# Seven block products for eight in the gates of the last 2048 tokens and in the output products of the last 1024

## The chip, the core and the metric

The kernel runs on one core of one Trainium2 chip. The metric is device microseconds of an execution; lower is better. The engines of the core are TensorE (PE, matmuls, with weight loads shown apart as PEld), VectorE (DVE), ScalarE (ACT), GpSimd (POOL) and SyncE (SP), which here issues nearly all the loads. All arithmetic is in 32-bit floating point; each wide product is made of three matmuls on a high and a low half in the type fp32r.

## The reference

For 4 batches, 8 heads, 768 positions and 64 values a head, attention over a window of 31 positions and over 24 summaries (of blocks of 32: the maximum of the keys, the mean of the values, with log 32 added to the score). The result, 3072 tokens of 512 values, goes through two gates and two matrices:

```python
scores_s = scale * np.einsum('bhsd,bhnd->bhsn', q, k_sum) + np.log(block)
scores_l = np.where(np.abs(pos[:, None] - pos[None, :]) < 16, scale * q @ k.T, -1e9)
a = softmax(concatenate([scores_l, scores_s]))      # the sum has 1e-9 added
x = a @ concatenate([v, v_sum])                     # 3072 x 512
h = (x @ w1) * (x @ w2) @ w3                        # 512 x 1024 each, 1024 x 1024
out = h @ w_out                                     # 1024 x 512
```

## The kernel before

The tokens are worked through in six **units** of 512. Heads come in four **pairs**, so there are 24 steps of attention, each one pair of one unit. The weights arrive as 64-bit words, are turned into floats on DVE and ACT (L150 to L190) and split into a high and a low half (`low`, L108). w3 and w_out are first folded into one matrix wp of 1024x512 (`fold_weights`, L196, 192 matmuls), eight tiles that stay in SBUF.

`products` (L111) is one wide product: high·high, low·high and high·low into one PSUM bank. `gate` (L427) makes one block of 128 columns of both gates for a unit: two banks of 4 × 3 matmuls; ACT copies the first (L448), DVE multiplies the second into it (L453), ACT casts the high half of the result (L454) and DVE makes its low half (L109). `project` (L459) makes 128 tokens of the output: 8 × 3 matmuls with wp into a bank that ACT copies out and stores itself (L472). A unit is 192 matmuls of gates and 96 of output, all 128x512.

Attention of a pair: scores (L331, 32 matmuls, tile sc), the mask and maximum on DVE (L345), the exponential on ACT (L359), its sum's reciprocal (L364 on POOL, L365 on DVE), the scaling on POOL (L368), then transposes on PE (L388, tile tp) copied to pt (L393, L397), and the product with the values (L408, tile po), which ACT and DVE turn into x (L419, L109). The loads of a pair are q, k (L306, L308) and v (L291) on SP; POOL copies the summary keys into k (L318) and the means of the values into v (L298).

The order of the work is written as a stream: `network` (L504) yields after each wide product, and `run(columns)` (L520) pulls it forward to a given sum of columns. In the first part, up to about 85 us, a table of numbered slots (`WORK`, `FIRST`) starts conversions and the first eight pairs. After it, a loop (L760 to L795) takes two pairs at a time: transposes of the two pairs before, scores of the two now, outputs of the two before, and then `run` for half a unit, 144 matmuls. In that part PE and POOL keep the order in which the program is written, and ACT and DVE do inside each step; SP does what the scheduler puts first. Every engine carries its own instructions out in order, and an SP issue that waits for a buffer holds those behind it.

In PSUM, tag mm has two banks (a gate or an output product each), tag tp two, and the scores have four.

Of the kernel before, what the change touches and what calls it, by code (L numbers as in the profile page):

```python
# [70 lines left out]
def attention_moe(ctx, tc, qG, kW, kT, vP, vW, vB, mask, w1, w2, w3T, wo, out):  # L71
# [17 lines left out]
    DO = out.shape[1]  # L89
    SCALE = 1.0 / math.sqrt(D)  # L90
# [15 lines left out]
    wp = [const.tile([P, 2, DO], F32R, name=f"wp{i}") for i in range(NF)]  # L106
# [142 lines left out]
    def value_means(b, c, raw):  # L249
        if c == 0:  # L250
            vs[b] = sb.tile([P, P], F32, name="vs")
        cols = vs[b][:, c * VC : (c + 1) * VC]
        nc.vector.tensor_reduce(out=cols, in_=raw, op=ALU.add, axis=AX.X)
        nc.vector.tensor_scalar(out=cols, in0=cols, scalar1=1.0 / BLOCK, scalar2=None, op0=ALU.mult)

# [59 lines left out]

    def gather(u, p, k):
# [46 lines left out]
    def invert(mx):  # L363
        nc.gpsimd.tensor_scalar(out=mx[:, 1], in0=mx[:, 1], scalar1=1e-9, scalar2=None, op0=ALU.add)  # L364
# [35 lines left out]
    def outputs(pt, v):  # L400

        po = ps.tile([P, 512], F32, name="po", tag="tp", bufs=2)
# [12 lines left out]
        return po  # L415

# [59 lines left out]
    NU = B * S // U  # L476
    NS = NU * NPAIR
# [25 lines left out]

    def network():  # L504
        for u in range(NU):
# [3 lines left out]
            for t in range(NBLK):  # L509
                yield from project(u, t, hs)  # L510

# [6 lines left out]
    given = [0.0]  # L518

    def run(columns):  # L520

        while given[0] < columns:
            n = next(stream, 0)
            if n == 0:
                return
            given[0] += n

# [30 lines left out]
    coming, loaded, turns, under_way = {}, {}, {}, []  # L558
    for b in range(1, B):
        steps = [(lambda c=c, b=b: load_blocks(b, c), lambda raw, c=c, b=b: value_means(b, c, raw)) for c in range(vB.shape[1])]  # L560
        steps += [
            (lambda p=p, b=b: load_keys(b, p), lambda raw, p=p, b=b: summaries(b, p, raw)) for p in range(NPAIR)
        ]
        if b == 1:
            of_second = steps
            continue
        at = b * BLOCKS // NBLK * NPAIR
        if at - 2 * NPAIR >= 2 * NPAIR:
            for i, some in enumerate((steps[:2], steps[4:6], steps[2:4], steps[6:])):
                turns[at - 2 * NPAIR + 2 * i] = some  # L570
            continue
        for at, step in zip((4, 4, 4, 4, 3, 3, 2, 2), steps):
            coming.setdefault(b * BLOCKS // NBLK * NPAIR - at, []).append(step)

    def prepare(s):
        for work, raw in loaded.pop(s, ()):
            work(raw)
        for load_, work in coming.pop(s, ()):
            loaded.setdefault(s + 1, []).append((work, load_()))

    def load_turn():
        if turns:
            under_way.extend((work, load_()) for load_, work in turns[min(turns)])

    def take_turn(s):
        if s in turns:
            del turns[s]
            for work, raw in under_way:
                work(raw)
            under_way.clear()  # L590
            load_turn()


# [70 lines left out]
    def means():  # L664
# [39 lines left out]
        41: [lambda: fetch_values(6), lambda: fetch_values(7), lambda: fill(6)],  # L704
        46: [lambda: fetch_sums(7)],
        47: [lambda: fill(7)],
        51: [lambda: fetch_sums(6)],
    }
    RATE = 8000
# [49 lines left out]
    with tc.manual_schedule(engines={engines.PE, engines.Pool}):  # L759
        for s in range(NFIRST, NS + 1, 2):  # L760
            now = (s, s + 1) if s < NS else ()
            last = (s - 2, s - 1)
            if s == NFIRST:
                for p in range(s, s + NPAIR):
                    prepare(p)
                load_turn()
# [95 lines left out]
```

## Time and profile before

| what | value |
|---|---|
| three runs | 532.22, 532.48, 535.3 us (median 532.48) |
| profiled execution, its span | 533.5 us, 1.0 above the median |
| PE busy | 511.2 us, 96% |
| DVE, ACT, POOL busy | 240.6, 225.4, 95.9 us |
| wide matmuls by line | 1152 gates, 576 output, 192 folding |
| moved by DMA | 68.78 MB |

The page shows an execution by busy time of each engine, and the chain that ended last; a group of instructions is given by line, engine, operation and tile, with count, busy time, mean duration and the idle time ahead. PE's busy time overlaps its weight loads. A view by windows gives the same for stretches of time, with the granted clock of TensorE and the DMA rate. For a transfer, the last number is the microseconds from its issue to its landing.

### The profile page before, as it was taken

The numbers are of one execution on the slowest core, as the hardware profiler recorded it, in microseconds if no ns is written. First come the engines' busy times: TensorE is split into PE (matmuls) and PEld (weight loads), VectorE is DVE, ScalarE is ACT, GpSimd is POOL, SyncE is SP. The second block draws the span as 40 slices with busy tenths as digits, with TensorE's granted clock in tenths as the row PEclk, the third lists the DMA queues.
The fourth block names the chain that finished last, engine by engine and source line by source line (L and its number), as shares of the span: only waits on it lengthen the run. The fifth ranks groups of instructions, "written<-read, shape, count | busy, mean of one in ns | idle before, by whom it ended". The sixth has DMA issues, their size and how long they took to land.

```text
span 533.5 us, 9766 instructions
## 1 busy us (share of the span) xinstructions
PE 511.2 (96%) x3888; PEld 421.4 (79%) x3888; DVE 240.6 (45%) x667; ACT 225.4 (42%) x627; POOL 95.9 (18%) x158
## 2 busy tenths in 40 slices
PE   1889989999999999999999999999999999999997
PEld 0667767888888888888888888888888888888885
DVE  5889987798534326435244043251042350222210
ACT  5587964674626226135154063361172361222210
POOL 2020635001033202305005014014023031000000
PEclk9989997999999999999999999999999999999999
DMA  8995699804834013453040150050150011100001
GB/s 346 413 411 220 252 325 413 316 2 139 274 131 167 0 55 122 151 172 134 0 177 1 60 195 1 1 177 20 49 187 2 14 69 40 39 3 0 1 20 59
DMA packets 21166, 68.78 MB, mean 129 GB/s; under 512 B 2304, under 2 KB 2432, under 8 KB 18560
## 3 DMA queue, kind: packets, MB, share of 16 engines
q1 hardware_dynamic: 17664, 61.86, 31.6%
q10 hardware_dynamic: 3456, 6.29, 3.1%
q8 instruction: 30, 0.49, 0.4%
q14 instruction: 16, 0.13, 0.1%
HBM read 61.85 MB, written 6.29 MB: 128 GB/s over the span
## 4 chain that ended last, share of the span: by engine, by line
PE 87%; DMA 5%; DVE 4%; ACT 2%; issue 1%; POOL 0%; SPq 0%; POOLq 0%; ACTq 0%
PE mm L113 76%; PE po L408 4%; PE sc L331 4%; DMA rows<-in_vP_dram 2%; PE tp L388 2%; DVE wf L176 2%; DMA wraw<-in_w_dram 1%; DVE w L109 1%; DMA wraw<-in_wo_dram 1%; ACT sm L359 1%; DVE wf L173 1%; ACT wf L164 1%; DVE sm L345 0%; ACT w L190 0%; DVE ks L236 0%
## 5 line engine op out<-in xcount | busy, mean ns | idle before, releaser
L113 PE MATMUL mm<-x,w 128*128 128x512 f32 x1152 | 264.3, 391 | 0.0
L113 PEld LDWEIGHTS mm<-x,w 128*128 128x128 f32 x1152 | 216.5, 188 | 45.3
L113 PE MATMUL mm<-wp,h 128*128 128x512 f32 x576 | 133.3, 390 | 0.0
L113 PEld LDWEIGHTS mm<-wp,h 128*128 128x128 f32 x576 | 107.7, 188 | 22.6
L359 ACT ACTIVATE sm<-sm,mx 128x120 f32<-128x120 f32 x192 | 73.6, 385 | 16.3 <-DVE mx L345 16.3
L453 DVE TENSOR_TENSOR g<-mm,g 128x512 f32<-128x512 f32 x48 | 33.1, 690 | 88.7 <-PE mm L113 85.4
L454 ACT CAST h<-g 128x512 fp32r<-128x512 f32 x48 | 29.5, 618 | 90.6 <-DVE g L453 90.6
L113 PE MATMUL mm<-w,w 128*128 128x512 f32 x192 | 51.2, 419 | 14.8 <-ACT w L190 12.0
L113 PEld LDWEIGHTS mm<-w,w 128*128 128x128 f32 x192 | 37.3, 200 | 25.7 <-ACT w L190 12.7
L364 POOL TENSOR_SCALAR mx<-mx 128x8 f32<-128x8 f32 x24 | 6.8, 283 | 275.5 <-ACT sm L359 275.3
L472 ACT COPY o<-mm 128x512 f32<-128x512 f32 x24 | 14.0, 584 | 82.5 <-PE mm L113 82.5
L397 DVE COPY pt<-tp 120x512 f32<-120x512 f32 x22 | 14.3, 684 | 75.2 <-PE tp L388 75.2
L109 DVE TENSOR_TENSOR h<-g,h 128x512 fp32r<-128x512 f32 x48 | 35.2, 736 | 25.6 <-ACT h L454 25.4
L448 ACT COPY g<-mm 128x512 f32<-128x512 f32 x48 | 28.1, 586 | 39.0 <-PE mm L113 38.4
L298 POOL COPY v<-vs 24x512 f32<-24x512 f32 (+1 forms) x64 | 40.7, 635 | 8.9 <-DMA v<-in_vW_dram 5.9
L345 DVE CUSTOM_DVE_ANT_0 sm<-sc,mask_sb 128x120 f32<-128x120 f32 x192 | 41.1, 274 | 0.0
L359 ACT ACTIVATION_READ_ACCUMULATOR sm<-sm,mx 128x1 f32 x192 | 36.2, 188 | 0.0
L368 POOL TENSOR_TENSOR sm<-sm,mx 128x960 f32<-128x960 f32 x16 | 28.7, 1793 | 5.6 <-DVE mx L365 5.6
L109 DVE TENSOR_TENSOR x<-po,x 128x512 fp32r<-128x512 f32 x24 | 16.6, 690 | 28.6 <-ACT x L419 28.5
L190 ACT CAST w<-wf 128x1024 fp32r<-128x1024 f32 (+1 forms) x22 | 21.3, 968 | 17.3 <-DVE wf L176 17.2
L408 PEld LDWEIGHTS po<-pt,v 120*64 120x64 f32 x768 | 24.5, 141 | 4.0 <-issue 2.5
L408 PE MATMUL po<-pt,v 120*64 120x64 f32 x768 | 26.6, 228 | 0.9 <-POOL v L298 0.5
(35 smaller groups left out, 287.9 us busy)
## 6 DMA issues: line engine op xcount, KB each, us to landing
v<-in_vW_dram SPq DMA_DIRECT2D x24, 512.0 KB, 6.4
wraw<-in_w3T_dram SPq DMA_DIRECT2D x8, 1024.0 KB, 13.0
wraw<-in_w_dram SPq DMA_DIRECT2D x8, 1024.0 KB, 9.3
k<-in_kW_dram SPq DMA_DIRECT2D x20, 368.0 KB, 5.3
raw<-in_kT_dram SPq DMA_DIRECT2D x16, 392.0 KB, 3.7
q<-in_qG_dram SPq DMA_DIRECT2D x24, 256.0 KB, 4.9
raw<-in_vB_dram SPq DMA_DIRECT2D x12, 512.0 KB, 3.8
out_dram<-o ACTq DMA_DIRECT2D x24, 256.0 KB, 2.0
```

The lines of the kernel that those rows point to most:

```text
L109: eng.tensor_tensor(dst, src, hi.bitcast(F32), ALU.subtract)
L113: nc.tensor.matmul(acc, lhsT=a, rhs=b, start=first and i == 0, stop=last and i == len(terms) - 1)
L190: nc.scalar.copy(t[:, 0, some], f[:, some])
L298: nc.gpsimd.tensor_copy(v[at : at + NB, g, blocks], src.unsqueeze(1).broadcast_to([NB, n, P]))
L331: nc.tensor.matmul(sc[h][64 * g : 64 * g + 64, i * KR : (i + 1) * KR], lhsT=q[rows, i * P + 64 * g : i * P + 64 * g + 64], rhs=k[rows, i, ...
L345: nc.vector.tensor_tensor_reduce(out=sm[:, j], in0=sc[h][:, i * KR : (i + 1) * KR], in1=mask_sb[:, 0 if blk == 0 else 2 if blk == BLOCKS - ...
L359: nc.scalar.activation(sm[:, j], sm[:, j], AF.Exp, bias=mx[:, 0, j : j + 1], scale=-1.0, accum_out=mx[:, 1, j : j + 1])
L368: nc.gpsimd.tensor_tensor(sm, sm, mx[:, 2].unsqueeze(2).broadcast_to([P, NI, KR]), ALU.mult)
L408: nc.tensor.matmul(po[cols, at : at + 64], lhsT=v[:KR, g, i, cols], rhs=pt[g][:, (h * NBLK + i) * 64 : (h * NBLK + i + 1) * 64], start=Tru ...
L448: nc.scalar.copy(g, a[:, :U])
L453: nc.vector.tensor_tensor(g, acc[1][:, :U], g, ALU.mult)
L454: nc.scalar.copy(h[:, 0], g)
```

## The change

The last 2048 tokens (units 2 to 5) go through the gates two units at a time. The input of such a pair of units and each 512 columns of the weights are cut into two by two blocks, and their product is made of seven block products of sums and differences where there were eight (`lanes`, k from 0 to 6). The x of these units stays in SBUF in plain floats (xraw, L449, a copy on ACT) and serves as the blocks. The differences of inputs are made on POOL in place (`difference`, L552 to L558), their halves on ACT (L562) and DVE (L118). The differences of weights are made once: POOL sums high and low half (L863 for the gates, L880 for wp), then takes the differences (L600 to L611), ACT casts (L591), DVE makes the low half (L118), and the result is stored in DRAM (L597) as wS (gates) and pS (output), 512 KB each; the plain halves are stored as they are (L853, L856). For each product two of them come back (`flow_in`, L666). `lanes` keeps four banks in the gates (tags mm and tp) and two in the output; each lane takes 6 matmuls of a k in the gates and 12 in the output, and after each k its bank is copied on ACT (k of 0 and 1, L691) or added to an earlier one on DVE (L694, L833). POOL multiplies the two gates (L697, 32 times).

Units 2 and 3 then have the plain output product (`project_split`), with wp read from DRAM; units 4 and 5 have the seven products (`project_fast`), and their output is stored transposed, into a second output that the host turns and appends. Units 0 and 1 stay as they were.

Attention now takes one pair at a time (`lump`): transposes, scores, 12 wide matmuls, outputs, then the rest of the pair's share, by the table `UP_TO`. A table `EXTRA` says at which pair weight sums, input differences and weight loads begin. The block means of values go to DRAM (`keep_means`, L329) and come into v by small transfers on SP (L335) instead of POOL copies; a part of the early pairs keeps the copies. The addition in `invert` moves from POOL to DVE (L385). wp lives in buffers that are given to other tiles later.

The core of the diff:

```diff
+    wS = [[tc.dram_tile([P, 2, KH * FQ], F32, name=f"wS{k}_{q}") for q in range(NQ)] for k in range(NK)]
+    pS = {k: [tc.dram_tile([P, 2, 2 * DH], F32, name=f"pS{k}_{c}") for c in range(NF // 4)] for k in range(2, NK - 1)}
+    pW = [tc.dram_tile([P, 2, DO], F32, name=f"pW{i}") for i in range(NF)]
+    vS = [tc.dram_tile([P, P], F32, name=f"vS{b}") for b in range(B)]
...
+    FIRST_OF_GROUP, LAST_OF_GROUP = (0, 2, 4), (1, 3, 6)
+    def source(k, b):
+        return b[(0, 1, 0, 1, 0, 0, 1)[k]][(0, 0, 0, 1, 0, 1, 0)[k]]
...
+    def difference(k, b):
+        src = source(k, b)
+        if k == 2:
+            nc.gpsimd.tensor_tensor(src, b[0][1], src, ALU.subtract)
+        elif k == 3:
+            nc.gpsimd.tensor_tensor(b[0][1], src, b[0][1], ALU.subtract)
+        elif k == 4:
+            nc.gpsimd.tensor_tensor(src, b[1][1], src, ALU.subtract)
+        elif k == 6:
+            nc.gpsimd.tensor_tensor(src, src, b[0][0], ALU.subtract)
...
+        def finished(k, raw):
+            to = sb.tile([P, 2, 512], F32R, name="sp", **home)
+            nc.scalar.copy(to[:, 0], raw)
+            yield 1
+            low(nc.vector, to[:, 1], raw, to[:, 0])
+            yield 1
+            yield 1
+            yield 1
+            nc.sync.dma_start(to_dram(k), to.bitcast(F32))
...
+        nc.gpsimd.tensor_tensor(a22, a21, a22, ALU.add)
+        yield 1
+        nc.gpsimd.tensor_tensor(a21, a11, a21, ALU.subtract)
+        works.append(finished(2, a22))
+        next(works[0])
+        yield 1
+        nc.gpsimd.tensor_tensor(a11, a22, a11, ALU.subtract)
+        works.append(finished(5, a21))
+        next(works[0])
+        next(works[1])
+        yield 1
+        nc.gpsimd.tensor_tensor(a12, a12, a11, ALU.subtract)
+        yield from staggered([*works, finished(4, a11), finished(3, a12)])
...
+    def flow_in(n):
+        while flow and len(ready) < n:
+            t = sb.tile([P, 2, 512], F32R, name="ws", tag="x", bufs=6)
+            flow.pop(0)(t)
+            ready.append(t)
...
+        banks = [ps.tile([P, 512], F32, name="ln", tag=tag, bufs=bufs) for tag, bufs in tags]
+        for k in range(NK):
+            stationary_of = yield from weights_of(k)
+            for i in range(n):
+                for c in range(steps):
+                    if between and c % KH == 0:
+                        between(k, i * steps // KH + c // KH)
+                    a, m = [stationary_of(i, c, w) for w in range(2)], moving_of(k, c)
+                    terms = [(a[0], m[0]), (a[1], m[0]), (a[0], m[1])]
+                    for j, (x, y) in enumerate(terms):
+                        nc.tensor.matmul(
+                            banks[i][:, :U],
+                            lhsT=x,
+                            rhs=y,
+                            start=c + j == 0 and k in FIRST_OF_GROUP,
+                            stop=c == steps - 1 and j == 2 and k in LAST_OF_GROUP,
+                            skip_group_check=True,
+                        )
+                    if c < steps - 1:
+                        yield 3 * U
+                with tc.high_priority(offset=SOONER):
+                    evacuated(k, i, banks[i][:, :U])
+                yield 3 * U
...
+                if k < 2:
+                    nc.scalar.copy(c11 if k else p1, got)
+                else:
+                    to, more = ((p5, p1), (c12, p1), (c12, c12), (p5, p5), (p1, p1))[k - 2]
+                    nc.vector.tensor_tensor(to, got, more, ALU.add)
+                if k >= 5:
+                    a, b = ((c12, p5), (c11, p1))[k - 5]
+                    nc.gpsimd.tensor_tensor(a, a, b, ALU.mult)
+                    finished.half(r, i, 6 - k, a)
+                finished.after(r, k, i)
...
+        EARLIER = {0: 2, 1: 3, 2: 4, 3: 6}
+        def between(k, j):
+            with tc.high_priority(offset=SOONER // 2):
+                if j == 0:
+                    if k in EARLIER:
+                        for b in blocks:
+                            difference(EARLIER[k], b)
+                    if k + 1 < NK:
+                        coming[:] = [halves(source(k + 1, b), d) for b, d in zip(blocks, whole.moving(k + 1))]
+                if j in (1, 2) and k + 1 < NK:
+                    for work in coming:
+                        next(work, 0)
...
+    def fetch_means(u, p, v):
+        for b, blocks, n in batches(u):
+            for g, at in enumerate((CUT, CUT - 64)):
+                src = vS[b][32 * p : 32 * p + NB]
+                nc.sync.dma_start(v[at : at + NB, g, blocks], src.unsqueeze(1).broadcast_to([NB, n, P]))
...
     def network():
-        for u in range(NU):
+        for u in range(2):
             hs = []
             for f in range(NF):
                 yield from gate(f, xs[u], hs)
             for t in range(NBLK):
                 yield from project(u, t, hs)
+        split = Split()
+        yield from gates(1, split)
+        yield from project_split(1, split)
+        tasks.extend(sums_of_output(c) for c in range(2))
+        whole = Whole(2)
+        yield from gates(2, whole)
+        yield from project_fast(2, whole)
...
+        run(given[0] + 12 * U)
+        with tc.manual_schedule(engines={engines.Activation, engines.DVE}):
+            finish_step(p - 2, pt, **more)
+            if b:
+                expose(0, sm, mx)
+                reduce(u, 1, sc, sm, mx)
+                expose(1, sm, mx)
+                invert(mx)
+                normalize(sm, mx)
+            fill(p + 1)
+            reduce_batch()
+        fetch_values(p)
+        for work in EXTRA.get(p, ()):
+            work()
+        run((given[0] + UP_TO[p]) / 2)
+        load_batch()
+        run(UP_TO[p])
```

**SP at the last pairs of unit 1.** In the loop of before, a step's issues on SP are the two pairs' q, k and v and nothing else:

```order
L306 DMA q_2777<-in_qG_dram 128x512
L308 DMA k_2778<-in_kW_dram 128x736
L306 DMA q_2783<-in_qG_dram 128x512
L308 DMA k_2784<-in_kW_dram 128x736
L291 DMA v_2401<-in_vW_dram 128x1024
L291 DMA v_2407<-in_vW_dram 128x1024
L306 DMA q_3141<-in_qG_dram 128x512
L308 DMA k_3142<-in_kW_dram 128x736
```

At the same place of the change (L317, L319 and L302 are q, k and v, L255 blocks of values, L335 means, L597 stores of weight differences, L666 loads of weight pieces):

```order
L597 DMA wS5_2_108<-sp_2622 128x1024
L597 DMA wS4_2_104<-sp_2708 128x1024
L302 DMA v_2765<-in_vW_dram 128x1024
L666 DMA ws_2773<-wS1_1_91 128x1024
L597 DMA wS3_2_100<-sp_2717 128x1024
L255 DMA raw_2789<-in_vB_dram 128x1024
L255 DMA raw_2791<-in_vB_dram 128x1024
L335 DMA v_2765<-vS2_132 24x4x128 x2
L317 DMA q_2813<-in_qG_dram 128x512
L319 DMA k_2814<-in_kW_dram 128x736
```

Stores and weight loads now stand between the loads of a pair, and each means transfer stands behind the load of its v.

**ACT at the start of unit 1.** In a step of before (the exponentials of a pair, the copies g of the first gate's bank, the casts h, the copy pt of transposes):

```order
L359 ACTIVATE sm_2475,mx_2476<-sm_2475,mx_2476 128x120 x5
L454 CAST h_2628<-g_2613 128x512
L359 ACTIVATE sm_2475,mx_2476<-sm_2475,mx_2476 128x120 x3
L448 COPY g_2645<-mm_2632 128x512
L454 CAST h_2628<-g_2645 128x512
L448 COPY g_2676<-mm_2663 128x512
L454 CAST h_2691<-g_2676 128x512
L448 COPY g_2708<-mm_2695 128x512
```

And in the change, after the last x of unit 0:

```order
L453 CAST x_1867<-po_1850 128x512
L380 ACTIVATE sm_1823,mx_1824<-sm_1823,mx_1824 128x120
L591 CAST sp_1934<-wr_1897 128x512
L380 ACTIVATE sm_1823,mx_1824<-sm_1823,mx_1824 128x120 x3
L591 CAST sp_1944<-wr_1897 128x512
L482 COPY g_1909<-mm_1893 128x512
L380 ACTIVATE sm_1823,mx_1824<-sm_1823,mx_1824 128x120 x4
L488 CAST h_1925<-g_1909 128x512
L591 CAST sp_1978<-wr_1897 128x512
```

The casts into sp, whose buffers hold data to be stored, now stand between the exponentials and the copies g that free a bank.

**PE in the gates of units 2 and 3.** Before, banks of the gates in turn (of the last unit; the gates of every unit read so):

```order
L113 MATMUL mm_4837<-x_4356,w12_919 128x512 x3
L113 MATMUL mm_4837<-x_4376,w12_919 128x512 x3
L113 MATMUL mm_4837<-x_4660,w12_919 128x512 x3
L113 MATMUL mm_4837<-x_4680,w12_919 128x512 x3
L113 MATMUL mm_4854<-x_4356,w12_902 128x512 x3
L113 MATMUL mm_4854<-x_4376,w12_902 128x512 x3
```

In the change, the start of the seven-product gates (ln is a lane's bank, xT an input difference, ws a weight piece, po the output of attention; of the output's eight rows the last is shown):

```order
L636 MATMUL ln_3020<-xT_3036,ws_2767 128x512 x6
L636 MATMUL ln_3021<-xT_3036,ws_2767 128x512 x6
L429 MATMUL po_3069<-pt_2988,v_2765 64x64 x2
L429 MATMUL po_3069<-pt_2989,v_2765 64x64 x2
L636 MATMUL ln_3022<-xT_3036,ws_2769 128x512 x6
L636 MATMUL ln_3023<-xT_3036,ws_2769 128x512 x6
L636 MATMUL ln_3020<-xT_3041,ws_2771 128x512 x6
```

Where before had 12 wide matmuls for one bank, a lane has 6 for one k, and the same bank ln_3020 returns with the next piece after three other lanes; one pair's output stands 12 matmuls after its scores.

More of the change, by code (lines that the diff above doesn't have):

```diff
@@ L398, in evacuate, with outputs @@
         return pt
-    def outputs(pt, v):
-        po = ps.tile([P, 512], F32, name="po", tag="tp", bufs=2)
+    def outputs(pt, v, **more):
+        po = ps.tile([P, 512], F32, name="po", **more or {"tag": "tp", "bufs": 2})
         for i in range(NBLK):
@@ L415, in outputs, with keep_raw @@
         return po
+    def keep_raw(po, u, c):
+        n, half = divmod(u, 2)
+        if (n, half) not in raws:
+            if half:
+                t = sb.tile([P, NC, U], F32, name="xraw", tag="w12", bufs=8)
+                raws[n, half] = [t[:, i] for i in range(NC)]
+            else:
+                home = {"tag": "wf", "bufs": 5} if n == 1 else {"tag": "raw", "bufs": 2}
+                two = [sb.tile([P, 2, U], F32, name="xraw", **home) for _ in range(NC // 2)]
+                raws[n, half] = [two[i // 2][:, i % 2] for i in range(NC)]
+        nc.scalar.copy(raws[n, half][c], po[:, :U])
     def keep_x(po, x):
@@ new lines, in attention_moe, with moving_x, start @@
+    xT, raws, hT, tasks = {}, {}, {}, []
+    def moving_x(n, k):
+        def start():
+            t = sb.tile([P, 2, KH, U], F32R, name="xT", tag="w12", bufs=8)
+            works = []
+            for c in range(KH):
+                b = [[raws[n, half][c + i * KH] if (n, half) in raws else None for half in range(2)] for i in range(2)]
+                works.append(moving(k, b, (t[:, 0, c], t[:, 1, c])))
+            yield from staggered(works)
+            xT[n, k] = t
+        tasks.append(start())
@@ new lines, in temporary, with __init__, temps, half @@
+    def temporary():
+        t = sb.tile([P, 2, U], F32, name="tmp", tag="wp", bufs=NF)
+        return t[:, 0], t[:, 1]
+    class Split:
+        def __init__(self):
+            self.h = {}
+        def temps(self, r, i):
+            return *temporary(), *temporary()
+        def half(self, r, i, u, raw):
+            f = 4 * r + i
+            if u == 1:
+                home = {"tag": "w12", "bufs": 8} if r else {"tag": "ring", "bufs": RING}
+                t = sb.tile([P, 2, 2, U], F32R, name="hs", **home)
+                self.h[f] = [[t[:, j, w] for w in range(2)] for j in range(2)]
+            h = self.h[f][u]
+            nc.scalar.copy(h[0], raw)
+            low(nc.vector, h[1], raw, h[0])
+        def after(self, r, k, i):
+            pass
@@ new lines, in finish_step, with work_on @@
+    def finish_step(p, pt, **more):
+        u, c = place(p)
+        po = outputs(pt, values.pop(p), **more)
+        if u < 2:
+            keep_x(po, xs[u])
+        else:
+            keep_raw(po, u, c)
+    def work_on(u, sm, mx, sc):
+        for h in range(2):
+            reduce(u, h, sc, sm, mx)
+            expose(h, sm, mx)
+        invert(mx)
+        normalize(sm, mx)
+    CLASSIC = ALL_FOLD + 2 * UNIT
+    FAST = 3 * U * 4 * KH
+    UP_TO = {p: TO_SLOTS + (CLASSIC - TO_SLOTS) * (p - NFIRST + 1) / NFIRST for p in range(NFIRST, 2 * NFIRST)}
```

316 lines of the change are left out of this document (241 added, 75 removed).

## The prediction

> **What bounds the kernel now.** I read the page first, for the share of each engine and of the last chain:
>
> ```profile
> span 533.5 us, 9766 instructions
> PE 511.2 (96%) x3888; PEld 421.4 (79%) x3888; DVE 240.6 (45%) x667; ACT 225.4 (42%) x627; POOL 95.9 (18%) x158
> DMA packets 21166, 68.78 MB, mean 129 GB/s; under 512 B 2304, under 2 KB 2432, under 8 KB 18560
> PE 87%; DMA 5%; DVE 4%; ACT 2%; issue 1%; POOL 0%; SPq 0%; POOLq 0%; ACTq 0%
> ```
>
> TensorE is busy 96% of the span and 87% of the last chain; nothing else has half. A busy PE can still be slow, so I read the chain in order of time, one step of the network (two pairs of heads) in the middle:
>
> ```profile
> 345.04 1.09 PE tp L388 x32
> 346.13 1.98 PE sc L331 x64
> 348.11 2.02 PE po L408 x64
> 350.12 32.87 PE mm L113 x144
> 462.38 67.60 PE mm L113 x297
> 530.00 0.59 ACT o L472
> ```
>
> A step is 5.09 us of attention and 144 wide matmuls in 32.87 us, one per 228.3 ns, with no wait. The last stretch, x297 in 67.60 us, keeps 227.6. Last I cut the span into stages (the columns: stretch, its length, busy time of PE, weight loads, DVE, ACT and POOL, then granted clock, DMA share and GB/s):
>
> ```profile
> 36.00:85.00 49.00, 45.44 (x479) 35.74 (x477) 43.79 (x98) 35.98 (x94) 17.45 (x24) 0.92 0.78 294
> 155.00:459.00 304.00, 303.93 (x2439) 253.93 (x2440) 105.53 (x380) 114.78 (x368) 60.37 (x90) 1.00 0.23 81
> 459.00:533.50 74.50, 70.72 (x393) 58.57 (x391) 13.75 (x20) 14.86 (x25) 0.00 (x0) 1.00 0.05 18
> 80.00:100.00 20.00, 18.97 (x145) 15.58 (x135) 13.95 (x16) 8.01 (x10) 7.37 (x11) 0.83 1.02 413
> 40.00:60.00 20.00, 20.00 (x194) 15.65 (x194) 19.04 (x52) 15.85 (x44) 4.90 (x5) 1.00 0.65 256
> ```
>
> From 155 us the clock is 1.00, PE has 0.07 us of idle time in 304, and DMA works at 81 GB/s. So a matmul taken away there is worth its whole 228 ns, as long as what replaces it stays hidden. The fourth row is what a full DMA system gives here, 413 GB/s; the last shows PE never idle beside a DVE that is 95% busy.
>
> **What is removed: 120 wide matmuls, −27.4 us.**
>
> ```profile
> L113 PE MATMUL mm<-x,w 128*128 128x512 f32 x1152 | 264.3, 391 | 0.0
> L113 PE MATMUL mm<-wp,h 128*128 128x512 f32 x576 | 133.3, 390 | 0.0
> ```
>
> These are six units of 192 and of 96. Units 2 to 5 do 7/8 of their gates, 4 × 192 × 7/8 = 672 for 768, and units 4 and 5 do 7/8 of their output, 168 for 192: 96 + 24 = 120 fewer. Each kept matmul still brings one weight load of 128x128, as in the rows of before, so the pace stays: 120 × 0.2283 = 27.4 us. That alone makes 506.1.
>
> **What stays on PE but is cut finer, +1.0 us.** Pairs come one at a time with 12 matmuls between the scores and the outputs. The rows of single pairs from the early part:
>
> ```profile
> 66.98 0.61 PE tp L388 x16
> 67.59 1.05 PE sc L331 x32
> ```
>
> Against half of 1.09 and of 1.98 that is 0.065 + 0.06 more per pair, 2.3 us for 18 pairs. Those rows lie where the mean clock was 0.92, which explains about half, so 1.0; bounds 0 and 2.3. At the end of unit 0 three blocks follow each other without matmuls between (transposes, scores, outputs), and unit 1 has nine matmuls (2.05 us) before it needs the x just made, whose cast and low half take 0.59 and 0.69 us behind other work: **+1.0**, bounds 0 and 1.5.
>
> **What is added on the vector engines.** The sums of blocks are new work of 128x512 pieces. Rows of the same form:
>
> ```profile
> L453 DVE TENSOR_TENSOR g<-mm,g 128x512 f32<-128x512 f32 x48 | 33.1, 690 | 88.7 <-PE mm L113 85.4 <-ACT sm L359 1.6 <-ACT wf L164 1.3
> L109 DVE TENSOR_TENSOR h<-g,h 128x512 fp32r<-128x512 f32 x48 | 35.2, 736 | 25.6 <-ACT h L454 25.4
> L454 ACT CAST h<-g 128x512 fp32r<-128x512 f32 x48 | 29.5, 618 | 90.6 <-DVE g L453 90.6
> L368 POOL TENSOR_TENSOR sm<-sm,mx 128x960 f32<-128x960 f32 x16 | 28.7, 1793 | 5.6 <-DVE mx L365 5.6
> ```
>
> With these (POOL per 512 columns scaled from 960: 0.96 us) DVE grows to about 300 us, ACT to 260, POOL to 173. By stage, counted from the order of the change: unit 1 has 93 us of PE work over 63 of DVE and 63 of ACT; the seven-product gates of units 2 and 3 have 99 over 62 and 53; everything after, 136 over 59, 39 and 41 of POOL. No engine reaches PE, and the window of 40 to 60 us shows DVE at 95% without a stall. Throughput costs nothing. Bank reuse is the other way in which it could: a lane's bank is needed again 18 matmuls (4.1 us) later in the gates and 12 (2.7 us) later in the fast output product; one copy or add of 0.69 us fits four times.
>
> **What can wait: order on ACT, DVE and POOL, +4 us.** A difference of weights is cast on ACT into a buffer whose last tenant must have been spilled to DRAM. ACT runs in order: behind the waiting cast stand copies that free a PE bank. The order leaves 2.1 to 5.3 us (12 casts, mean 3.9, 8 of them among attention) between the spill's issue and the next cast, and two banks give PE another 2.7. The nearest rows for a transfer of 512 KB, steady stage first, then the first 100 us with the queues full:
>
> ```profile
> v<-in_vW_dram SPq DMA_DIRECT2D x16, 512.0 KB, 6.3
> k<-in_kW_dram SPq DMA_DIRECT2D x14, 368.0 KB, 4.5
> out_dram<-o ACTq DMA_DIRECT2D x17, 256.0 KB, 2.0
> v<-in_vW_dram SPq DMA_DIRECT2D x6, 512.0 KB, 9.6
> k<-in_kW_dram SPq DMA_DIRECT2D x4, 368.0 KB, 6.8
> ```
>
> At 6.3 the median cast is 6.3 − 3.9 − 2.7 = 0.3 us inside its cover; with 9.6 each of the 8 costs 3.0, 24 us in all. The load here lies between (280 GB/s, below, against 81 and 345), nearer the steady row once PE has slack: 0.5 us each, 4 us; bounds 0 and 24. POOL's gather of summary keys has 2.7 to 3.3 us after its load's issue, and lands at 4.5; SP waits for a value tile before it may issue the small transfers of means. Both feed blocks a whole step later, so I cost them at nothing; without that cover each would add 1.5 us per pair, inside the same bounds.
>
> **What is added on DMA, +3 us.** Counted from the order, the traffic goes from 68 to 142 MB: weight pieces of 512 KB spilled once and read back for every product, and wp read again. From the first single pair to the fast output it is 85.3 MB in about 304 us of PE work, 280 GB/s. SP issues 303 transfers for 123, at 0.33 to 0.43 us each. The dense place is the last part of unit 1 and the start of the seven-product gates: 15.8 MB in 42.4 us, 372 GB/s. Most weight pieces are issued 12 to 20 us of PE work ahead, but the scores of the first pair there have 6.6 us from the issue of their k, and the pieces of product 2 have 8.5 and 9.6, all behind spills and block loads on the one SP queue. At 413 GB/s nothing is late; at 294, the second window, the stretch takes 53.7 us and PE waits 11.3. The mean of the first 100 us is the value between:
>
> ```profile
> DMA packets 7994, 34.49 MB, mean 345 GB/s; under 512 B 835, under 2 KB 963, under 8 KB 5427
> ```
>
> At 345 the stretch takes 45.8, 3.4 us late; I take +3, bounds 0 and 11. The Trainium skill (DMA: Bandwidth & Descriptors, Specifications) gives about 358 GB/s as what a core gets from HBM; the window from 80 us moved 413, so the trace is above it. By 358 the stretch would need 44.1 us, 1.7 late, and the sum would be 1.3 us lower.
>
> **The end, +1.5 us.** The window from 459 us has 3.8 us without PE work, at the last pair's outputs and after the last matmul (0.59 us of copy and a store of 2.0). The change ends with an add of 0.69 and an SP store, and has three changes of stage (gates to output and back) at which PE needs a first product's inputs and PSUM banks of another tag: 0.5 each, bounds 0 and 4.
>
> **Sum against the profiled execution:** 533.5 − 27.4 + 1.0 + 1.0 + 4 + 3 + 1.5 = 516.6. The profiled span is 1.0 above the median of the runs (532.5), so **516 us**, 3.1% less. What a measurement of this kernel tells from no change is about 1%.
>
> **Rivals.** *All hidden* (0.22): every wait inside its cover, as 6.3 us landings and 413 GB/s would have it; 506.1 less the profile's 1.0 is 505, with the finer cuts 507; 505 to 509. Against it: twelve casts with 5.3 us or less.
>
> *SP's queue and the in-order waits cost more* (0.18): landings of 8 us under load instead of 6.3: 8 casts × 1.4 = 11 us for 4, and 7 for 3 of DMA: 527. For it: SP has been held at a single tile already (start, us until it could go on):
>
> ```profile
> 35.66 16.28 SPq L291 DMA_DIRECT2D v<-in_vW_dram  x2
> ```
>
> Against it: that stage had 294 GB/s of demand, and the change puts few such waits ahead of urgent loads.
>
> *DVE held by POOL* (0.06). Before's timeline shows it (start, duration):
>
> ```profile
> 207.03 1.79 POOL L368 TENSOR_TENSOR sm<-sm,mx 128x960 f32<-128x960 f32 x1 [0.81 <-DVE mx L365]
> 207.52 1.85 DVE L109 TENSOR_TENSOR h<-g,h 128x512 fp32r<-128x512 f32 x1
> ```
>
> The DVE subtraction takes 1.85 us for its usual 0.69 and ends 0.55 us after POOL has ended (208.82). The change adds 96 such subtractions (32 of before's go) and 104 POOL operations on 512 columns or more. In the fast output, a product of 5.5 us has four subtractions and four POOL differences, 2.8 + 3.8 = 6.6 us if none overlap, in four products of seven: 4.4 us. Of the 68 others, one in six 1.16 us later and a third of that on the path is another 4: 524. The Trainium skill (SBUF — State Buffer, SBUF: two separate sides) says that a DVE operation with two SBUF inputs and a POOL operation exclude each other for a whole instruction; the row agrees.
>
> *Bound by DMA, slower than before* (0.11). The place is the whole part from the first single pair to the fast output, and the price is its 85.3 MB. If the rate delivered, with SP's in-order waits in it, is below 85.3 / (304 + 27.4) = 257 GB/s, the gain is gone. At 250 it takes 341 us, 37 more than PE: 506 + 37 = 543, 542 as a run's time. For it: the window from 40 us, with loads outstanding, gave only 256. Against it: SP was held there (the row above), and a full queue gave 413.
>
> **How the numbers follow.** The forecast's own case, 510 to 523, has 0.43; with the cases above this makes 1.00. Faster by over 1% (below 527) is the forecast's case, all hidden, DVE held, and a third of the SP case: 0.43 + 0.22 + 0.06 + 0.06 = 0.77; within 1% gets the rest of the SP case, 0.12, and slower 0.11. The low end, 506, leaves out half of all hidden (0.1); the high end, 531, leaves out the DMA case. So 506 to 531.
>
> **What would show it.** Right: 1800 wide matmuls, the stretches of 42 matmuls at 228 ns with clock 1.00, windows of the seven-product gates with PE over 97% busy, SP holds below 5 us. Wrong: PE idle put down to loads of weight pieces (DMA case), to ACT copies of a bank behind a cast of a sum (in-order case), or to DVE subtractions of 1.2 us and more (POOL case); wide matmuls at another pace would break the first term.

## The result, and the profile after

The change makes the kernel slower: 548.59 us median of four runs (546.5 to 549.19) beside 532.94 for the kernel before; the ratio is 1.028 (95% interval 1.025 to 1.031). The forecast was 516 us, 506 to 531. The profiled execution of the change has a span of 544.7 us; it is the shortest of its four runs (546.5) and that of before the longest of its four (535.3), so that the spans lie 11.2 us apart where the medians lie 15.7. Its page, to be set against that of before:

```profile
span 544.7 us, 10211 instructions
...
PE 499.8 (92%) x3768; PEld 399.0 (73%) x3768; DVE 350.2 (64%) x797; ACT 254.5 (47%) x687; POOL 224.9 (41%) x198
...
DMA packets 48961, 142.93 MB, mean 262 GB/s; under 512 B 5136, under 2 KB 11792, under 8 KB 46352
...
PE 66%; DVE 15%; POOL 6%; ACT 5%; DMA 5%; issue 2%; SPq 0%; POOLq 0%; ACTq 0%; DVEq 0%
```

The 120 matmuls are gone (3888 to 3768), and PE is busy 11.4 us less, but it now stands idle for 44.9 us where it stood for 22.3. Of the last chain 87% were PE; now 66% are, and 26% belong to DVE, POOL and ACT, which had 6%. POOL's busy time has grown from 95.9 to 224.9 us, well past the 173 that I had counted, and DVE's to 350 past my 300. Most of that second excess is no work that I had left out: of the 120 subtractions of 512 columns on DVE 43 took over 0.8 us, each of them beside a two-input operation on POOL, and what they took beyond 0.69 us adds up to 38 us (in before to 2).

Where PE waits is read from the waits by engine, here those of the weight loads that go ahead of matmuls, after 150 us:

```profile
...
PEld mm L122 <- ACT g L482: 5.3, 1, 5.3
PEld ln L636 <- ACT tmp L830: 5.1, 1, 5.1
...
PEld po L429 <- ACT pt L414: 4.8, 3, 1.8
PEld po L429 <- DVE pt L418: 4.2, 3, 2.0
...
PEld ln L636 <- DVE tmp L833: 2.4, 2, 1.4
```

No row of this view names a transfer. They are few and long: one wait of 5 us for a copy that frees a gate's bank, another of 5 us in the output product, and pairs of 1 to 2 us at the attention blocks. Placed in time, by adding up how far the starts of neighbouring matmuls lie beyond 226.5 ns (gaps over 0.12 us, after 150 us):

| stretch, us | excess, us | place |
|---|---|---|
| 156 to 162 | 3.0 | last two pairs of unit 0 |
| 193 to 196 | 1.3 | outputs in unit 1 |
| 219 to 231 | 8.0 | sums of the gates' weights |
| 306 to 323 | 6.9 | products of the gates, units 2 and 3, first half |
| 364 to 374 | 5.6 | the same, second half |
| 499 to 521 | 8.1 | gates of units 4 and 5 to their output |

Together 32.9 of the 36.5 us that such gaps make there; in before they made 2.8. In the first 150 us they shrank from 16.2 to 12.9, and gaps under 0.12 us grew by 7.7 over the whole span. With the 120 matmuls: −27.2 + 33.7 − 3.3 + 7.7 = 10.9 of the 11.2 us between the two spans; the rest lies behind the last matmul. These are estimates: the split between long and short gaps moves by some 3 us with the pace that one takes for the short matmuls of attention. The −3.3 need not be the change's doing: the profiled execution of before ran 10.2 us of its first 87 at half clock, and that of the change none.

The third row, followed back in the chain of waits (start, duration, what):

```profile
208.04 5.60 DMA k<-in_kW_dram
...
213.76 0.06 POOL k L339
...
214.42 2.38 POOL wr L863
216.80 1.75 POOL sm L389
218.55 2.33 POOL wr L863
...
220.95 1.27 POOL wr L600
...
222.28 1.27 POOL wr L602
...
224.11 0.59 ACT g L482
...
224.74 8.56 PE mm L122 x24
```

and ACT in the same stretch, with its idle time and what ended it in brackets:

```profile
222.24 0.62 ACT L591 CAST sp<-wr 128x512 fp32r<-128x512 f32 x1 [7.67 <-POOL wr L600]
223.58 0.62 ACT L591 CAST sp<-wr 128x512 fp32r<-128x512 f32 x1 [0.73 <-POOL wr L602]
224.11 0.58 ACT L482 COPY g<-mm 128x512 f32<-128x512 f32 x1
```

POOL first waits for a late k, then does four sums or differences (L863 twice, L600, L602) and a scaling; ACT waits 7.67 us for the third of them, L600, because its next instruction is the cast of that sum; the copy g, for which PE waits, stands behind two such casts though its bank had long been full. And the 24 matmuls that follow take 8.56 us where 24 × 0.228 is 5.5: the clock had been halved, as the granted clock shows, the third number from the end (the columns are those of the windows in the prediction).

```profile
224.00:230.80 6.80, 6.06 (x14) 4.85 (x15) 6.12 (x22) 5.31 (x19) 5.50 (x4) 0.50 0.86 294
...
247.00:290.00 43.00, 43.00 (x415) 34.25 (x414) 35.91 (x109) 29.12 (x97) 19.69 (x20) 1.00 0.90 322
```

The second of these rows is the dense stretch of loads at the start of the seven-product gates. It moved 322 GB/s and PE did not stand still at all.

The last row of the table, in the same chain:

```profile
484.87 0.70 DVE tmp L694
485.64 1.30 POOL hr L697
...
487.01 1.30 POOL hr L554
488.31 1.25 POOL hr L697
...
489.63 1.29 POOL hr L554
...
496.13 1.26 POOL hr L697
...
497.42 0.63 ACT hT L562
...
498.07 1.11 DVE hT L118
...
504.43 5.03 PE ln L636 x15
```

Products of the gates and differences for the next product take turns on POOL, 1.3 us each, back to back for 12 us. The lanes of the gates finish faster than that (one in 6 matmuls, 1.37 us, against two POOL operations), so when the gates end the inputs of the output product are not there.

The prices behind it, by form, first after the change:

```profile
L697 POOL TENSOR_TENSOR hr<-hr,tmp 128x512 f32<-128x512 f32 x16 | 20.8, 1307 | 44.0 <-DVE tmp L694 43.4
...
L118 DVE TENSOR_TENSOR xT<-xraw,xT 128x512 fp32r<-128x512 f32 x28 | 32.6, 1196 | 7.0 <-ACT xT L562 6.9
...
L118 DVE TENSOR_TENSOR hT<-hr,hT 128x512 fp32r<-128x512 f32 x28 | 29.0, 1067 | 15.2 <-ACT hT L562 14.9
```

A POOL operation with two full inputs of 512 columns takes about 1.3 us, not the 0.96 that I had scaled from the 960-column row. That is its price while no subtraction on DVE runs beside it, as in the chain above to 497 us; the 96 of the change took 1.43 on average and up to 2.08. The subtraction on DVE beside it takes 1.07 to 1.20 us on average, where e4 below has it at 0.69 with POOL idle.

### The profile page after: what moved, and what is told of

Same layout as the page of the kernel before. It is cut to its first block, busy times and chain, and to the rows that moved or that the text cites. A ratio compares the mean times of both kernels' runs of the same rounds, so it can differ in the third digit from the quotient of the medians.

```text
span 544.7 us, 10211 instructions
## 1 busy us (share of the span) xinstructions
PE 499.8 (92%) x3768; PEld 399.0 (73%) x3768; DVE 350.2 (64%) x797; ACT 254.5 (47%) x687; POOL 224.9 (41%) x198
## 4 chain that ended last, share of the span: by engine, by line
PE 66%; DVE 15%; POOL 6%; ACT 5%; DMA 5%; issue 2%; SPq 0%; POOLq 0%; ACTq 0%; DVEq 0%
PE ln L636 27%; PE mm L122 22%; PE lo L122 8%; PE po L429 4%; PE sc L352 3%; DVE hT L118 2%; DVE wf L185 2%; POOL tmp L697 2%; DVE w L118 2%; PE tp L409 2%; DVE hs L118 2%; POOL hr L697 1%; ACT sm L380 1%; DVE wf L182 1%; DMA wraw<-in_w_dram 1%
## 5 line engine op out<-in xcount | busy, mean ns | idle before, releaser
L636 PE MATMUL ln<-xT,ws 128*128 128x512 f32 x672 | 158.8, 395 | 1.3 <-DVE tmp L694 1.3
L636 PEld LDWEIGHTS ln<-xT,ws 128*128 128x128 f32 x672 | 125.8, 189 | 29.9 <-DVE tmp L694 2.4
L122 PE MATMUL mm<-x,w 128*128 128x512 f32 x384 | 90.5, 393 | 0.1
L122 PEld LDWEIGHTS mm<-x,w 128*128 128x128 f32 x384 | 71.2, 188 | 16.1 <-issue 0.6
L694 DVE TENSOR_TENSOR tmp<-ln,tmp 128x512 f32<-128x512 f32 x64 | 43.4, 685 | 26.8 <-PE ln L636 26.7
L122 PE MATMUL mm<-wp,h 128*128 128x512 f32 x192 | 48.7, 412 | 4.8 <-ACT g L482 4.8
L122 PE MATMUL lo<-ws,hs 128*128 128x512 f32 x192 | 47.1, 402 | 1.4 <-DVE tmp L694 1.4
L122 PEld LDWEIGHTS mm<-wp,h 128*128 128x128 f32 x192 | 37.6, 199 | 13.9 <-ACT g L482 5.3
L636 PE MATMUL ln<-hT,ws 128*128 128x512 f32 x168 | 40.5, 401 | 6.2 <-ACT tmp L830 4.6
L122 PEld LDWEIGHTS lo<-ws,hs 128*128 128x128 f32 x192 | 36.3, 193 | 10.1 <-DVE tmp L694 2.2
L389 POOL TENSOR_TENSOR sm<-sm,mx 128x960 f32<-128x960 f32 x16 | 29.6, 1850 | 29.0 <-DVE mx L386 11.0
L697 POOL TENSOR_TENSOR hr<-hr,tmp 128x512 f32<-128x512 f32 x16 | 20.8, 1307 | 44.0 <-DVE tmp L694 43.4
L118 DVE TENSOR_TENSOR hT<-hr,hT 128x512 fp32r<-128x512 f32 x28 | 29.0, 1067 | 15.2 <-ACT hT L562 14.9
L118 DVE TENSOR_TENSOR sp<-wr,sp 128x512 fp32r<-128x512 f32 x24 | 19.0, 805 | 30.4 <-ACT sp L591 30.4
L429 PEld LDWEIGHTS po<-pt,v 120*64 120x64 f32 x768 | 25.1, 140 | 17.1 <-issue 6.0
L562 ACT CAST hT<-hr 128x512 fp32r<-128x512 f32 x28 | 16.8, 622 | 44.6 <-POOL hr L697 33.1
```

The lines of the kernel that those rows point to most:

```text
L118: eng.tensor_tensor(dst, src, hi.bitcast(F32), ALU.subtract)
L122: nc.tensor.matmul(acc, lhsT=a, rhs=b, start=first and i == 0, stop=last and i == len(terms) - 1)
L389: nc.gpsimd.tensor_tensor(sm, sm, mx[:, 2].unsqueeze(2).broadcast_to([P, NI, KR]), ALU.mult)
L429: nc.tensor.matmul(po[cols, at : at + 64], lhsT=v[:KR, g, i, cols], rhs=pt[g][:, (h * NBLK + i) * 64 : (h * NBLK + i + 1) * 64], start=Tru ...
L562: nc.scalar.copy(dst[0], src)
L636: nc.tensor.matmul(banks[i][:, :U], lhsT=x, rhs=y, start=c + j == 0 and k in FIRST_OF_GROUP, stop=c == steps - 1 and j == 2 and k in LAST_ ...
```

## The experiments

Three theories went into them. **A**: POOL's two-input operations pace a chain that runs in order over POOL, ACT and DVE, and PE waits at its end. **B**: loads are late, DMA is the bound. **C**: DVE is short of time. Times are medians; before, on the same chips, was 532.5 to 533.3 in all batches.

**e1, the products on DVE.**

```diff
-                    nc.gpsimd.tensor_tensor(a, a, b, ALU.mult)
+                    nc.vector.tensor_tensor(a, a, b, ALU.mult)
```

> The 32 products of the two gates (L697) move from POOL to DVE. Theory A (POOL's two-input operations, 1.3 us each, are the slow member of an in-order chain POOL, ACT cast, DVE low half that ends at PE): the stalls of PE at 306 to 324 us (6.9 us with the half clock behind it) and at 364 to 374 us (5.6 us) go, and about half of the 8.1 us around 500 to 521; 548.6 - 14 to 17 = 532 to 535 us. Theory B (loads arrive late, DMA is the bound): the loads are the same, 546 to 551 us. Theory C (DVE, busy 64% and held by POOL, is short of time): 22 us more work on DVE, 550 us or more.

Measured 538.05 us (nine runs), 10.5 faster than the change, ratio to before 1.009 (1.006 to 1.012), 3 us above the range of A. The stalls at 306 to 323 and 364 to 374 us shrank from 12.5 us to 1.9, but the long one near 500 us stayed:

```profile
PE mm L122 <- ACT g L482: 4.7, 1, 4.7
PE ln L636 <- DVE tmp L833: 3.8, 1, 3.8
```

B and C fall by the sign; A has the direction, but expected half of the stall near 500 us to go. What is left there hangs on more than POOL's own price. In the chain behind the second of these waits stand four subtractions on DVE of 1.70 us each, beside POOL's differences, which take 1.70 themselves (first the row of POOL, then the piece of the chain):

```profile
499.36 5.11 POOL L556 TENSOR_TENSOR hr<-hr 128x512 f32<-128x512 f32 x3
...
499.86 6.81 DVE hT L118 x4
```

At 0.69 each they would have been done 4.0 us sooner, an estimate, and the wait is 3.8.

**e2, the gates' weight sums on DVE** (the same edit in five lines: L600, L602, L606, L611, L863).

> The sums and differences of weights (L600 to L611, L863) move from POOL to DVE; the products and the differences of inputs stay on POOL. Theory A: only the stall at 219 to 231 us goes, 5.0 us of wait and 2.9 us of half clock: 539 to 542 us. Theory B: 546 to 551 us. Theory C: slower in the part from 160 to 260 us, 552 us or more.

Measured 543.12 us, 5.5 faster, ratio 1.016 (1.011 to 1.021). The stall at 219 to 231 is gone, but scores wait 2.8 us near 250, and the three small gaps near 158 us were followed by half clock here. The direction is as A said, the time 1.1 us above its range.

**e6, the differences of inputs and the sums of wp on DVE** (the same edit in L552 to L558 and L880).

> The third part alone: the differences of inputs (L552 to L558) and the sums of wp (L880) on DVE, the sums of the gates' weights and the products on POOL as in the change. Theory A (each stall has its own chain through POOL): the stall at 219 to 231 us stays (8 us), the two at 306 to 324 and 364 to 374 shrink a little, the 8 us from 499 to 521 shrink by about half, since the products still pace the last gates: 538 to 543 us, so that the three parts alone add up to the 25 us of all. Rival (one stall causes the next, so the parts do not add): 546 us or more.

Measured 547.82 us, ratio 1.027 (1.023 to 1.031): not to be told from the change, a miss for A as I had put it, and inside the range of its rival. The wait near 500 us was still there, 4.1 us. The products on POOL still take 1.3 us for each lane, and the differences, now on DVE, are held beside them, 1.2 to 1.8 us for most:

```profile
490.95 1.30 POOL hr L697
...
492.27 2.35 DVE hr L554 x2
```

**e4, all of them on DVE.**

```diff
-        nc.gpsimd.tensor_tensor(a22, a21, a22, ALU.add)
+        nc.vector.tensor_tensor(a22, a21, a22, ALU.add)
...
-            nc.gpsimd.tensor_tensor(src, b[0][1], src, ALU.subtract)
+            nc.vector.tensor_tensor(src, b[0][1], src, ALU.subtract)
```

> All two-input additions and products of 512 columns that the change brought move from POOL to DVE (L552 to L558, L600 to L611, L697, L863, L880); POOL keeps copies and the scaling of the probabilities. Theory A: the stalls from 219 us on go nearly all, 28 us: 520 to 526 us, PE busy over 97% from 200 to 480 us. Theory B: 546 to 551 us. Theory C: DVE gets 80 us more work and has 430 of 545 us; the stalls stay under another name, 545 to 560 us.

Measured 523.11 us, 25.5 faster than the change and faster than before: ratio 0.981 (0.978 to 0.984). Two lines of its page, and the waits of PE after 150 us:

```profile
span 521.4 us, 10193 instructions
...
PE 491.4 (94%) x3768; PEld 395.6 (76%) x3768; DVE 381.7 (73%) x901; ACT 255.4 (49%) x687; POOL 70.1 (13%) x94
```

```profile
PE sc L352 <- DVE vs L263: 3.7, 1, 3.7
PE tp L409 <- DVE x L118: 1.2, 1, 1.2
PE po L429 <- ACT pt L414: 1.1, 1, 1.1
```

After 260 us no wait over 1.0 us is left; the 3.7 are scores near 250 us. DVE has more to do than ever, 381.7 us, and that costs nothing: C falls. Its subtractions are back at their price beside an idle POOL, and stretched only for xT, which still meets the 16 scalings:

```profile
L118 DVE TENSOR_TENSOR hT<-hr,hT 128x512 fp32r<-128x512 f32 x28 | 18.1, 687 | 6.4 <-ACT hT L562 6.4
...
L697 DVE TENSOR_TENSOR hr<-hr,tmp 128x512 f32<-128x512 f32 x16 | 10.9, 691 | 0.3
...
L118 DVE TENSOR_TENSOR xT<-xraw,xT 128x512 fp32r<-128x512 f32 x28 | 26.1, 960 | 10.6 <-ACT xT L562 10.5
```

The three parts alone gave 10.5 + 5.5 + 0.8 = 16.8, all together 25.5. The 8.7 between could be the stall near 500 us (8.1), if either the products or the differences on POOL are enough to keep it, as the two chains above suggest. The next one tells.

**e13, products and differences on DVE, the gates' weight sums on POOL** (e1 and e6 together).

> Products, differences of inputs and the sums of wp on DVE; only the sums and differences of the gates' weights stay on POOL. Moved alone, the products gave 10.5 us and the differences 0.8, all three parts together 25.5. Theory A (the stalls around 500 to 521 us hang on products and differences both, and go only when both leave POOL): no wait over 1.5 us after 300 us, the 5 us wait near 215 to 231 us stays with its half clock, 528 to 531 us. Rival (the gain beyond the parts comes from POOL being idle as a whole): the wait near 500 us stays, 535 to 538 us.

Measured 529.44 us (twelve runs), ratio 0.995 (0.992 to 0.997): 19.2 faster than the change, where e1 and e6 alone make 11.3. The wait near 500 us is gone; the one for the copy g stays, with 6.8 us of half clock behind it:

```profile
PE mm L122 <- ACT g L482: 4.8, 1, 4.8
PE po L429 <- DVE pt L418: 1.7, 3, 0.8
```

So the two belong to one stall, and from here to e4 the weight sums give 6.3, as they gave 5.5 alone.

**e5, half of the weight pieces not loaded** (the low half of the 72 pieces is left out and the high half used in its place, so the output is not the reference's).

```diff
-        flow.extend(lambda t, k=k, r=r, i=i: nc.sync.dma_start(t.bitcast(F32), wS[k][2 * r + i]) for r in range(NF // 4) for k in range(NK) for i in range(2))
+        flow.extend(lambda t, k=k, r=r, i=i: nc.sync.dma_start(t.bitcast(F32)[:, 0], wS[k][2 * r + i][:, 0]) for r in range(NF // 4) for k in range(NK) for i in range(2))
...
-        return lambda t: nc.sync.dma_start(t.bitcast(F32), pW[i])
+        return lambda t: nc.sync.dma_start(t.bitcast(F32)[:, 0], pW[i][:, 0])
...
```

> Leaves out the low half of every weight piece that is read back (56 pieces of the gates, 16 of wp for the plain output): 18.9 MB less to load, the high half is used in its place, so the output is not the reference's; every instruction elsewhere stays. Theory A: the stalls do not hang on these loads, 545 to 549 us. Theory B: the part bound by DMA gets a fifth less to move, at least 10 us faster, 538 us or less. Theory C: as A.

Measured 552.4 us, ratio 1.034 (1.028 to 1.040): 18.9 MB less, and not faster, so B falls, as it does by e4, which loads as much as the change. It is 3.8 us slower than the change, and its trace has a wait that the change does not have, the one that I had forecast for it: a cast behind a spill on its way to DRAM, and a copy of a bank behind the cast. PE then waited 4.84 us for the copy o of 264.77.

```profile
261.34 0.62 ACT L591 CAST sp<-wr 128x512 fp32r<-128x512 f32 x1 [5.29 <-DMA wS<-sp]
...
264.77 0.59 ACT L506 COPY o<-mm 128x512 f32<-128x512 f32 x1
```

**e12, the plain output product** on top of e4: units 4 and 5 get eight products like units 2 and 3.

```diff
-        whole = Whole(2)
-        yield from gates(2, whole)
-        yield from project_fast(2, whole)
+        split = Split()
+        yield from gates(2, split)
+        yield from project_split(2, split)
...
```

> On top of all sums on DVE, the output of the last 1024 tokens is made with eight products, as in before (24 wide matmuls more; the sums of wp and the inputs' differences for it go). If a wide matmul is worth its 228 ns once no chain through POOL is left: 5.5 us slower than with the seven products, 528 to 530 us. If the seven products of the output cost in waits and stores what they save: 521 to 525 us.

Measured 529.11 us (ten runs, 526.6 to 532.8), 6.0 above e4 for 24 matmuls more, 250 ns each. That agrees with 228 ns a matmul once nothing else holds PE; the scatter is too wide, and the sums and stores that went with the edit too many, to tell 228 from 250.

Four kernels on top of e4 went for the waits that it has left: 3.0 us at 156 to 162 us and the 3.7 near 250.

**e7, more of unit 0 kept for later.**

```diff
-    TO_SLOTS = ALL_FOLD + 0.96 * UNIT
+    TO_SLOTS = ALL_FOLD + 0.92 * UNIT
```

> On top of all sums on DVE: 0.92 instead of 0.96 of unit 0 is done before the single pairs start, which leaves 23 wide matmuls for 11 between the blocks of the last two pairs of unit 0. If the 3 us of PE waits at 156 to 162 us are the want of matmuls between these blocks: 520 to 521 us. If taking them from the first part uncovers conversions there instead: 523 us or more.

Measured 525.25 us, 521.51 to 527.86, where e4 had 522.78 to 525.4: no gain. The excess near 160 us stayed, 3.3 us, now all at the outputs instead of at the transposes too. The matmuls between the blocks were not what it lacked; what it lacks was not settled.

**e8, q and k of units 2 to 5 issued by ACT**, and **e9**, e7 and e8 together.

```diff
-        nc.sync.dma_start(q, qG[p, :, u * U : (u + 1) * U])
+        eng = nc.scalar if u > 1 else nc.sync
+        eng.dma_start(q, qG[p, :, u * U : (u + 1) * U])
...
```

> On top of all sums on DVE: q and k of units 2 to 5 are issued by ACT and not by SP, where they stand behind stores and weight pieces. If the one stall left at 247 to 254 us (3.9 us of wait and 1.1 us of half clock, scores whose k was issued 4.5 us ahead) is the late k: 517 to 519 us. If an issue on ACT that waits for a free buffer holds ACT's copies: 524 us or more.

> All sums on DVE, with both of the changes before (0.92 of unit 0 first, q and k issued by ACT). If the two stalls are independent and each falls as said: 514 to 517 us, which is 506 us of span without waits plus 7.6 us of finer cuts.

Measured 527.17 and 531.15 us: both slower than e4, and e9 far from the 514 to 517 expected. e8 lies in the range given for copies held by an issue on ACT, but for another reason. Its scores no longer wait for k, and at the same place PE waits 4.3 us for a copy o that stands on ACT behind a cast whose buffer waits for its spill:

```profile
255.72 0.62 ACT L592 CAST sp<-wr 128x512 fp32r<-128x512 f32 x1 [3.53 <-DMA wS<-sp]
256.24 0.58 ACT L415 COPY pt<-tp 120x512 f32<-120x512 f32 x1
256.72 0.59 ACT L507 COPY o<-mm 128x512 f32<-128x512 f32 x1
```

**e10, the scaling of the probabilities on DVE too** (L389).

> On top of all sums on DVE: the scaling of the probabilities (L389, 16 times 1.84 us on POOL) on DVE too, 1.17 us each, so that POOL has only small copies. If DVE and POOL still hold each other up (the low halves xT take 0.96 us for 0.69 beside these 16): xT back at 0.69 us, the 3.9 us wait at 247 us gone, 518 to 521 us. If DVE, then near 77% busy, is what comes next: stalls under DVE's name in the steps of one pair, 525 us or more.

Measured 527.38 us (seven runs). xT is back at 686 ns from 960, so the two engines do hold each other up, but it did not pay: the scores near 250 us wait 4.2 us, now with POOL itself waiting for the k load.

**e11, two weight pieces called in early instead of four.**

```diff
-        14: [gates_flow, lambda: flow_in(4)],
+        14: [gates_flow, lambda: flow_in(2)],
```

> On top of all sums on DVE: two weight pieces instead of four are called in at the end of unit 1, so that more of the six shared buffers are free for the sums on their way to DRAM. If the waits left there (ACT's casts behind spills, 14.8 us of ACT's idle time) decide: 518 to 521 us. If they are covered, or if the late pieces are waited for instead: 523 to 527 us.

Measured 526.49 us, the second of the two cases: the pieces came late.

```profile
PE ln L636 <- DMA ws<-wS: 4.1, 1, 4.1
```

e4, e8, e10 and e11 have each one wait of 3.7 to 4.3 us at the same place, between 245 and 265 us, under four names: in e4 scores whose k POOL had gathered only after other work (the weight load's row names that gather, 3.9 us, where the row shown names DVE), then a spill, a k, a weight piece. What was moved forward there brought another thing late. It is not so in every execution: in the trace of e7, taken of the shortest of its runs, PE waits no longer than 1.1 us between 235 and 270 us, and in that of e12 2.2. The place is the dense stretch of SP's queue; what would clear it was not found.

## Why the prediction was wrong, point by point

**What bounds the kernel.** Right: PE, and a matmul at 228 ns. After the change 294 wide matmuls in a row took 66.65 us, 226.7 ns each, and e12 puts 24 of them at 6.0 us for a forecast 5.5, with a scatter of several us. The −27.4 us stand as far as this shows.

**"Throughput costs nothing", vector engines.** The claim holds for DVE (e4 gives it 31 us more than the change and is 25.5 us faster). For POOL it failed, and this is the step that broke the forecast. I priced POOL's work at 0.96 us per 512 columns from a row whose second operand is one value for a whole block of columns; with two full inputs it is 1.29, and 1.43 on average with the holding by DVE. POOL's total came to 225 us for 173. More than that, I compared sums by stage (41 of 136 us) and did not look at the rate where the work arrives: in the last gates a lane brings one product and one difference, 2.6 us of POOL, every 1.37 us. A sum over a stage cannot show this.

The Trainium skill had a nearer row: GPSIMD Engine Reference, section 3.1, has a two-input addition of 2048 columns on POOL at 4497 ns, 1.96 times the time of DVE, limited by a read port that the two inputs share. Here it was 1307 against 691 ns for the same product, 1.89 times, in the change and in e4. The page's ratio on DVE's 0.69 us would have given 1.35 us, an estimate, against 0.96 from the 960-column row.

**"What can wait: order on ACT, DVE and POOL, +4 us."** The place was right and the thing waited for was wrong. I had the cast of a sum on ACT with a bank's copy behind it, and had it wait for a spill; in the change it waits 7.67 us for POOL's addition. It waits for spills too, 12.5 us over seven casts of wS, but no wait of PE in the list is put down to one. In e5 and e8 the spills do bite, with 4.3 to 4.8 us each. The term was 4; by the experiments the chains through POOL are worth 25.5, a little above its upper bound of 24. The sign that the prediction gave for this case, ACT's copy of a bank behind the cast of a sum, did come.

**DVE held by POOL.** A rival with 0.06 and 524 us. Its mechanism is in the traces (1067 to 1196 ns on average for 690), its sign came, and it is part of theory A: e4 removes the price of POOL's operations and the holding together. By place they can be told apart to some extent. To 497 us POOL runs back to back at 1.3 us beside adds on DVE that stay at 0.69, so there its own duration decides; in the chain of 208 to 224 us no subtraction on DVE stands at all. From 498 to 521 us both are stretched, and what e1 left there is mostly the holding. At 306 to 323 and 364 to 374 us the chain has both. How much of the 25.5 us belongs to each was not measured.

**"What is added on DMA, +3 us."** Too high for the change: the dense stretch moved 322 GB/s without a stall, and e5 with 18.9 MB less is not faster. The rival that forecast the right side, slower by DMA, did so for a reason that did not hold. What the traces show of it is the late k of 208 us, 5.6 us from issue to landing, and a v of 4.71 us at 299, each at the head of a chain through POOL, and the one wait left in e4.

**"Cut finer, +1.0 us" and +1.0 at the end of unit 0.** Too low. Gaps under 0.12 us grew by 7.7 us, and by as much in e4, so they belong to the order and not to the stalls. By the starts of the matmuls a change between kinds of work on PE costs some 0.1 to 0.2 us, and there are about 50 more of them; the rest is spread over the wide matmuls. How much each makes was not settled. The end of unit 0 took 3.0 for 1.0.

**Not in the prediction at all: the clock after a stall.** The change runs 17.1 us at half clock (6.8 at 224 us, 3.4 each at 319, 371 and 504), always at a wait, which is worth up to 8.5 us; in its three other runs the granted clock was 0.978 for 0.984, so there was more of it, 12 us lost by that share (an estimate). Before had 10.2 us of it, all in its first 87 us. The traces show it behind single waits of 3.7 and 4.9 us and behind pairs of 1.4 to 2 us close together (312 to 319 us), and the three gaps of 156 to 162 us brought it in e2 and e5 but not in the change. The Trainium skill (TensorE: Matmul & The Clock Gate, Why this matters for your kernels) asks for no idle gap over about 3 us. The waits of 3.7 and more agree, and so does one of 2.2 in e12 without half clock behind it; in e2 one of 2.8 brought it, and the pairs show that here shorter ones can do it too.

**The sum again, with what was measured:** 533.5 − 27.2 for the matmuls, + 33.7 for gaps over 0.12 us after 150 us, + 7.7 for smaller ones, − 3.3 for a start at full clock, + 0.3 at the end: 544.7. I had 10.5 for all of it together but the first term.

## What to carry to other kernels

When a change buys matmuls with additions, price each addition on its engine from a row with the same operands, count what it holds up on the engine beside it, and set the rate at which the work arrives against that price at the tightest place, not the sums over a stage. On engines that work in order, ask of each new instruction what it waits for and what stands behind it: here casts of sums, which nobody needed for tens of microseconds, stood ahead of copies on which PE waited. And a stall of 4 us costs PE up to another 3 at half clock.

The version with all sums on DVE (e4) is the better kernel: 523.1 us, 1.9% under before.

## What the runs showed of the hardware that was not expected

- A two-input operation of 128x512 in 32 bits took 691 ns on DVE (e4) and 1307 on POOL (the change); with 1024 columns it took 2.3 to 2.5 us on POOL.
- A second operand that is one value for each block of 120 columns went with a lower price on POOL: 1793 ns for 960 columns is 1.87 ns a column (before), two full inputs were 2.55 (the change).
- All 43 subtractions of 512 columns that took over 0.8 us on DVE in the change ran beside a two-input operation on POOL, and POOL's took up to 2.08 us for 1.29.
- From 150 us to the last matmul half clock came in stretches of 3.4 or 6.8 us. In the change each began within a microsecond of PE's return from a wait.
